# Reading a result back into SBUF for two output blocks, and a new instruction order for a two-branch spectral kernel on one core

## The chip, the cores and the metric

One core of a Trainium2 chip runs the whole kernel. The metric is the device time of one execution in microseconds (us). The core has five engines with a queue each: TensorE (PE in the profile; PEld is its weight load), VectorE (DVE), ScalarE (ACT), GpSimd (POOL) and SyncE (SP), which here only issues DMA transfers. Each queue is worked off in the order in which the program was written. An instruction whose inputs are not there holds up all that stand behind it in its queue.

## The reference

Two branches work on sequences of 2048 steps by 640 channels and are mixed by a gate:

```python
x = A_q
g = _sigmoid((x * gate_w).sum(-1, keepdims=True))
# branch A: short convolution of k (4 taps), times v, long causal convolution with ssm_k by FFT, times q
k_shift = sum over 4 taps of k_pad[:, t:t + S, :] * shift_k
kv = k_shift * v
y = irfft(rfft(kv, 2 * S) * rfft(ssm_k, 2 * S))[:S] + kv * ssm_D
a = q * y
# branch B: two-dimensional FFT of the input, times a complex filter, and back
b = irfft2(rfft2(x) * (w_r + 1j * w_i))
return g * a + (1 - g) * b
```

Branch B takes `x = A_q` as its input too. Everything is float32.

## The kernel before, in words

All Fourier transforms are written as matmuls with constant matrices, in two stages each, with a 32x32 block transpose on DVE (`STREAM_TRANSPOSE`) that moves each stage's result from PSUM back to SBUF. The work is cut into units, and a unit's name with its number and the number of the step in it names every instruction below (`afin9.4` is step 4 of unit 9 of `afin`).

- **Start of branch B.** `fwd` (8 units, lines 286 to 319) folds one eighth of the input by four additions in SBUF (steps 1, 2 at L295 and 3, 4 at L297), multiplies it on PE (L303, L310), and ACT brings the result back into XX. `gcol` (L278 to L282) makes the gate's columns by five tiny DVE operations; every `fwd` matmul waits for it. `gate` (L328) gathers the gate when all eight `fwd` are done. `b1` (10 units, L348, L352) is the first stage of the long transform.
- **Middle of branch B.** `bs2` (8 units, L369 to L379) is the second stage: two matmul groups, four DVE products with the filter w (L374), two combining additions (L378). Each unit loads its w into one of two L buffers. `i1` (6 units) and `u` (16 units) go back, and `dic` (8 units, L430 to L458) ends branch B: matmuls, scaling by 1-g on ACT, four additions in SBUF (L448, L450), and two transfers to the output: columns 0 to 383 are added onto what branch A has stored there (an accumulating transfer, issued by POOL, L454), columns 384 to 639 are stored plainly by SP (L457).
- **Branch A** goes by five column blocks c = 0 to 4. `kv` (10 units, two a block) makes kv (PE L469, DVE L472, two additions L478, a transpose L481), `h` (10 units) loads the filter (an accumulating load, L489) and adds the D term (L491), `s1Y` and `s1H` are first stages (L509, L519), `s2` (20 units, four a block) multiplies spectra (PE L539, ACT L544, products L557 and L560, for blocks 1 and 3 additions L565), `is1` goes back (L265, L270), and `afin` (10 units, two a block, L582 to L613) ends it: PE L600, one product with g times q (L606, from PSUM on DVE), and the output.

Blocks 0, 1, 2 of branch A are stored first and branch B is added onto them. For blocks 3 and 4 it is the other way: branch B is stored first (L457), and each of the four `afin` units 6 to 9 adds its 512 KB by an accumulating transfer that POOL issues (L612).

Three tables set everything that is free. `ORDER` is the order in which the planned operations are written, and so the order in each queue. `ON_DVE` names the SBUF operations made by `ttop` that go to DVE; the others go to POOL. `SLOTS` gives each buffer its place in its pool (five V, four M, three T, two L, two H, one G, eight PSUM banks). The durations handed to `op` and the `kb` are read by nothing in the program:

```python
with tc.manual_schedule():
    for i in ORDER:
        plan.ops[i].fn()
```

Of the kernel before, what the change touches and what calls it, by code (L numbers as in the profile page):

```python
# [7 lines left out]
OP = mybir.AluOpType  # L8
# [17 lines left out]
    "bs2": [(7, 8)],
    "s2": [(3, 4), (4, 9), (4, 11), (6, 4), (7, 4), (7, 9), (8, 9), (9, 9), (10, 9), (12, 4), (12, 9), (13, 4), (13, 9), (14, 4), (14,
        9), (14, 10), (14, 11), (15, 4), (15, 9), (16, 4), (16, 9), (17, 4), (17, 9), (19, 4)],
    "afin": [(0, 4), (1, 4), (3, 4), (4, 4), (5, 4), (6, 4), (7, 4), (8, 4), (9, 4)],
    "dic": [(0, 6), (0, 8), (1, 6), (1, 7), (1, 8), (2, 6), (2, 9), (4, 6), (4, 7), (4, 8), (4, 9), (5, 6), (5, 8), (5, 9), (7, 7)],  # L30
    "kv": [(7, 5), (8, 5), (9, 5)],
# [713 lines left out]
```

## Time and profile before

| | us |
|---|---|
| median of three runs | 324.7 (319.17, 324.7, 324.92) |
| the profiled execution, its own time | 325.14 |
| its span, first to last instruction | 323.3 |
| PE busy | 259.7 (80% of the span) |
| DVE busy | 237.7 (73%) |
| POOL busy | 160.6 (50%) |
| ACT busy | 103.7 (32%) |
| mean granted PE clock | 0.946 |

The time is 1.84 us longer than the span in the profiled execution. A group in the profile is named by its line, engine and operation, then output and inputs by buffer name; a bracket behind an instruction in the timeline is the idle time just before it and what ended it.

### The profile page before, as it was taken

What the parts mean: (1) busy time and instruction counts of PE and PEld (TensorE: products, weight loads), DVE (VectorE), ACT (ScalarE), POOL (GpSimd) and SP (SyncE); (2) the same over time, 40 slices, a digit from 0 to 9 for tenths busy, and PEclk for the clock granted to TensorE, in tenths of its full rate; (3) what the DMA queues carried; (4) which work ended last, traced back from release to release, by engine and by line L of the source; (5) the groups of instructions that cost most, each with busy time, mean ns of one, the idle gap of its engine ahead of it and who ended that gap; (6) DMA issues with size and microseconds to landing.
All of it is one profiled execution on the core that took longest, in us unless ns stands there. A gap on an engine that the chain in (4) does not pass through costs nothing. (4 is left out here: it accounts for less than half of the span.)

```text
span 323.3 us, 10329 instructions
## 1 busy us (share of the span) xinstructions
PE 259.7 (80%) x4626; PEld 151.5 (47%) x4626; DVE 237.7 (73%) x241; ACT 103.7 (32%) x233; POOL 160.6 (50%) x120
## 2 busy tenths in 40 slices
PE   0399979988989769887669589888999987999920
...
DVE  2919965988989798998867697227846878797730
...
GB/s 291 418 415 358 396 274 35 310 415 258 39 153 317 149 131 3 2 188 356 256 152 191 138 2 212 307 143 243 233 107 129 178 160 109 67 74 14 2 148 112
DMA packets 26172, 60.49 MB, mean 187 GB/s; under 512 B 1680, under 2 KB 16400, under 8 KB 24464
## 3 DMA queue, kind: packets, MB, share of 16 engines
...
q8 instruction: 36, 0.59, 0.7%
q14 instruction: 8, 0.07, 0.1%
...
## 5 line engine op out<-in xcount | busy, mean ns | idle before, releaser
L519 DVE STREAM_TRANSPOSE YY<-banks 128x1024 f32<-128x1024 f32 x40 | 48.2, 1229 | 11.5 <-PE banks L509 11.5
L539 PE MATMUL banks<-YY,s2a 64*32 64x256 f32 x1280 | 46.7, 417 | 9.3 <-DVE M L557 4.0
L478 POOL TENSOR_TENSOR T<-V 128x512 f32<-128x512 f32 x13 | 18.2, 1436 | 45.9 <-DVE V L472 45.9
L539 PEld LDWEIGHTS banks<-YY,s2a 64*32 64x32 f32 x1280 | 25.9, 110 | 31.2 <-DVE YY L519 7.6
L544 ACT ACTIVATE H<-banks 128x512 f32<-128x512 f32 x40 | 23.9, 598 | 39.5 <-PE banks L539 30.6
L303 PE MATMUL banks<-cc,XX 128*64 128x162 f32 (+1 forms) x256 | 22.7, 325 | 14.6 <-DVE cc L282 12.2
L590 ACT ACTIVATE V<-V,g 128x128 f32<-128x128 f32 x72 | 22.0, 389 | 38.1 <-DMA V<-q 26.8
L265 PE MATMUL banks<-YY,ca 32*64 32x512 f32 x512 | 33.2, 607 | 0.8 <-DVE YY L519 0.5
L557 POOL TENSOR_TENSOR YY<-YY,H 128x512 f32<-128x512 f32 x15 | 19.6, 1315 | 17.8 <-ACT H L544 13.0
L303 PEld LDWEIGHTS banks<-cc,XX 128*64 128x64 f32 x256 | 19.0, 147 | 20.0 <-POOL XX L297 12.7
L270 DVE STREAM_TRANSPOSE YY<-banks 128x2048 f32<-128x2048 f32 x10 | 23.1, 2310 | 5.1 <-PE banks L265 5.1
L374 DVE TENSOR_TENSOR M<-banks,L 128x642 f32<-128x642 f32 x32 | 24.4, 813 | 2.8 <-DMA L<-w 2.7
L600 PE MATMUL banks<-YY,is2a 128*64 128x128 f32 x320 | 21.3, 291 | 4.8 <-DVE YY L270 2.5
L600 PEld LDWEIGHTS banks<-YY,is2a 128*64 128x64 f32 x320 | 19.5, 143 | 10.0 <-DVE YY L270 4.0
L472 DVE TENSOR_TENSOR V<-banks,V 128x1024 f32<-128x1024 f32 x10 | 12.1, 1210 | 15.4 <-DMA V<-v 6.7
L265 PEld LDWEIGHTS banks<-YY,ca 32*64 32x64 f32 x512 | 14.6, 129 | 17.9 <-issue 10.7
L430 PE MATMUL banks<-di,L 128*128 128x160 f32 x128 | 20.6, 316 | 2.5 <-ACT L L419 2.4
L378 POOL TENSOR_TENSOR XX<-M,M 128x642 f32<-128x642 f32 x15 | 19.8, 1384 | 5.2 <-DVE M L374 3.4
L297 POOL TENSOR_TENSOR XX<-M 128x640 f32<-128x640 f32 x10 | 18.3, 1842 | 7.8 <-DVE M L295 7.5
L430 PEld LDWEIGHTS banks<-di,L 128*128 128x128 f32 x128 | 18.5, 198 | 7.2 <-ACT L L419 4.7
L419 ACT ACTIVATE L<-banks 128x640 f32<-128x640 f32 x16 | 11.1, 703 | 33.0 <-PE banks L411 28.9
L348 PE MATMUL banks<-XX,cb 128*128 128x512 f32 (+1 forms) x42 | 20.6, 629 | 1.3 <-DVE M L557 1.0
...
## 6 DMA issues: line engine op xcount, KB each, us to landing
...
V<-v SPq DMA_DIRECT2D x10, 512.0 KB, 7.4
V<-h SPq DMA_DIRECT2D x10, 512.0 KB, 7.0
V<-h POOLq DMA_DIRECT2D x10, 512.0 KB, 8.3
V<-q SPq DMA_DIRECT2D x10, 512.0 KB, 4.8
out_dram<-V SPq DMA_DIRECT2D x6, 512.0 KB, 5.7
```

The source lines that it names most:

```text
L265: mm(p[h * 64:h * 64 + 64, j, :nd * 8], is1[r, sg, ri, :], v[r, h * 2 + src, :, d0:d0 + nd, :].rearrange("p m d e -> p d m e"), start=(i = ...
L270: nc.vector.transpose(by_col(x, d0, nd), p[:, :, :nd * 8].rearrange("p j (d i) -> p d j i", i=8))
L303: mm(bk(p, g_)[ri * 64:ri * 64 + 64, o:o + n], X[:, s, g_ * 64:g_ * 64 + 64], df[:, 0, ri * 323 + o:ri * 323 + o + n], start=(o == 0), sto ...
L348: mm(v()[:, e0:e0 + ne], m1b, by_col(XX, d0 + e0, ne), start=True, stop=True)
L374: op("DVE", dve(642), lambda x=x, t=t, ri=ri, p=p: tt(T(t)[:, ri], ps(p)[:, :, :NC], sb(w_, 2, 2, NC)[:, x], op=OP.mult), r=[p, w_], w=[t] ...
L378: ttop(642, lambda f, ri=ri, o=o, dst=dst: f(dst(), T(t1)[:, ri], T(t2)[:, 1 - ri], op=o), r=[t1, t2], w=xe + [("XS", m, e, ri)])
L430: mm(bk(p, b)[:, n * 160:n * 160 + 160], U[:, t_, r_], di[:, b * 160:b * 160 + 160], start=(n == 0), stop=False)
L519: op("DVE", dve(1024), lambda b=b: nc.vector.transpose(by_col(YY[:, :, y], a * 64 + b * 32, 32), view(b)), r=[p[b]], w=yk)
L539: mm(ps(p)[j * 32:j * 32 + 32, h].rearrange("p (y r d) -> p y r d", y=2, r=2)[:, :, ri], s2a[r, k, ri * 32:ri * 32 + 32], YY[r, k // 2, y0 ...
L544: op("ACT", act_us(512), lambda p=p, hs=hs: act(sb(hs, 2, 256), ps(p)[:, :, 256:], AF.Copy), r=[p], w=[hs])
L590: act(dst(j), src(j), AF.Copy, scale=g[:, n0 + j:n0 + j + 1])
L600: mm(v()[b * 64:b * 64 + 64, j, :], is2a[:, n2, :], row(YY[:, :, yp], n2), start=True, stop=True)
```

## The change

For two of the last four `afin` units (7 and 9, the second halves of blocks 3 and 4) the accumulating transfer goes. Instead SP reads back what branch B has stored (512 KB into a V buffer), DVE adds it in SBUF, and SP stores the sum plainly. Units 6 and 8 keep the accumulating transfer. `ON_DVE`, `ORDER` and `SLOTS` are all new. Of the SBUF additions, DVE now has 24 of the 32 of `fwd` (16 before), 6 of the 16 of `kv` (3), 16 of the 32 of `dic` (15), 9 of the 16 combining ones of `s2` (3), and none of `bs2` (1). The other edits to numbers are durations that nothing reads.

```diff
 ON_DVE = {(n, i, k) for n, l in {
-    "fwd": [(0, 1), (1, 1), (1, 2), (1, 3), (1, 4), (2, 1), (2, 4), (3, 4), (4, 1), (4, 2), (5, 1), (6, 1), (6, 4), (7, 1), (7, 2), (7,
-        4)],
...
+    "fwd": [(0, 1), (0, 2), (0, 3), (1, 1), (1, 2), (1, 3), (1, 4), (2, 1), (2, 2), (2, 3), (2, 4), (3, 1), (3, 3), (3, 4), (4, 1), (4,
+        4), (5, 3), (6, 1), (6, 3), (6, 4), (7, 1), (7, 2), (7, 3), (7, 4)],
...
+    "afin": [(0, 4), (2, 4), (3, 4), (4, 4), (5, 4), (6, 4), (7, 4), (7, 6), (8, 4), (9, 4), (9, 6)],
...
+BACK={7,9}
...
         if c < FIRST:
             op("SP", ISS, lambda: dma(out[:, n0:n0 + 8, cs], Q()), r=[qt], w=[("oA", c, n0 // 8)], kb=524)
+            return
+        ob = [("oB", v) for v in range(n0 // 2, n0 // 2 + 4)]
+        if 2 * c + n0 // 8 in BACK:
+            bt = new("V")
+            op("SP", ISS, lambda: dma(sb(bt, 8, 128), out[:, n0:n0 + 8, cs]), r=ob, w=[bt], kb=524)
+            ttop(1024, lambda f: f(sb(qt, 1024), sb(qt, 1024), sb(bt, 1024), op=OP.add), r=[bt], w=[qt])
+            op("SP", ISS, lambda: dma(out[:, n0:n0 + 8, cs], Q()), r=[qt, bt], kb=524)
         else:
-            op("POOL", 1.4, lambda: nc.gpsimd.dma_start(out[:, n0:n0 + 8, cs], Q(), accum_op=OP.add),
-               r=[qt] + [("oB", v) for v in range(n0 // 2, n0 // 2 + 4)], kb=800)
+            op("POOL", 1.6, lambda: nc.gpsimd.dma_start(out[:, n0:n0 + 8, cs], Q(), accum_op=OP.add), r=[qt] + ob, kb=1150)
```

The lines of the changed program stand two to three higher up to `kv` and `s2` (L295 is L297, L297 is L299, L374 is L376, L606 is L609), and the accumulating transfer of `afin` is L622.

Three places show what the new order does. First the start of the DVE queue. Before, `gcol` (`cc` and `gt`) stands behind the first addition of each of two units:

```order
L295 TENSOR_TENSOR M_64<-XX 128x640
L295 TENSOR_TENSOR M_65<-XX 128x640
L278 TENSOR_SCALAR cc<-cc 128x8
L279 TENSOR_TENSOR gt<-cc 128x2x2
L280 TENSOR_TENSOR gt<-cc 128x2x2
L281 TENSOR_TENSOR cc<-gt 128x2x2
L282 TENSOR_TENSOR cc<-gt 128x2x2
L297 TENSOR_TENSOR XX<-M_64 128x640
```

In the changed program the first unit (`fwd6`) is folded as far as DVE does it ahead of `gcol`:

```order
L297 TENSOR_TENSOR M_64<-XX 128x640
L297 TENSOR_TENSOR M_65<-XX 128x640
L299 TENSOR_TENSOR XX<-M_64 128x640
L297 TENSOR_TENSOR M_66<-XX 128x640
L299 TENSOR_TENSOR XX<-M_64 128x640
L280 TENSOR_SCALAR cc<-cc 128x8
L281 TENSOR_TENSOR gt<-cc 128x2x2
L282 TENSOR_TENSOR gt<-cc 128x2x2
L283 TENSOR_TENSOR cc<-gt 128x2x2
L284 TENSOR_TENSOR cc<-gt 128x2x2
L297 TENSOR_TENSOR M_66<-XX 128x640
```

Three more additions and the wait for one more input stand ahead of `gcol` now; POOL's queue holds one addition of `fwd6` and then one of `fwd0`, which needs DVE additions that stand behind `gcol`.

The second place is DVE in `bs2`, at the first reuse of an L buffer. Before, from the last product of `bs22` (buffer L_63) to the first of `bs21` in the same buffer, with all of `bs20` (L_62), two `s2` products and one long transpose (L270) between:

```order
L374 TENSOR_TENSOR M_65<-banks,L_63 128x642
L560 TENSOR_TENSOR YY<-banks,H_77 128x4x128
L374 TENSOR_TENSOR M_66<-banks,L_62 128x642
L560 TENSOR_TENSOR YY<-banks,H_76 128x4x128
L374 TENSOR_TENSOR M_66<-banks,L_62 128x642
L374 TENSOR_TENSOR M_67<-banks,L_62 128x642 x2
L270 STREAM_TRANSPOSE YY<-banks 128x64x16x2
L374 TENSOR_TENSOR M_64<-banks,L_63 128x642 x2
```

In the changed program the same stretch goes from the last product of `bs20` (L_62) to the first of `bs21` in that buffer:

```order
L376 TENSOR_TENSOR M_66<-banks,L_62 128x642
L376 TENSOR_TENSOR M_65<-banks,L_63 128x642
L563 TENSOR_TENSOR YY<-banks,H_76 128x4x128
L376 TENSOR_TENSOR M_65<-banks,L_63 128x642
L376 TENSOR_TENSOR M_67<-banks,L_63 128x642 x2
L376 TENSOR_TENSOR M_64<-banks,L_62 128x642
```

Four products of the other buffer and one `s2` product now stand between two uses of one buffer.

The third place is the end of the DVE queue, `is1` (L270, L272) and the four `afin` units. Before:

```order
L557 TENSOR_TENSOR YY<-banks,H_77 128x4x128
L270 STREAM_TRANSPOSE YY<-banks 128x64x16x2 x3
L606 TENSOR_TENSOR V_68<-banks,V_68 128x1024
L606 TENSOR_TENSOR V_69<-banks,V_69 128x1024
L606 TENSOR_TENSOR V_71<-banks,V_71 128x1024
L606 TENSOR_TENSOR V_70<-banks,V_70 128x1024
```

In the changed program (L619 is the new addition):

```order
L609 TENSOR_TENSOR V_68<-banks,V_68 128x1024
L272 STREAM_TRANSPOSE YY<-banks 128x64x16x2 x2
L609 TENSOR_TENSOR V_70<-banks,V_70 128x1024
L619 TENSOR_TENSOR V_70<-V_70,V_69 128x1024
L609 TENSOR_TENSOR V_71<-banks,V_71 128x1024
L609 TENSOR_TENSOR V_72<-banks,V_72 128x1024
L619 TENSOR_TENSOR V_72<-V_72,V_68 128x1024
```

And the end of SP's queue there, behind the last loads of q (L589) and branch B's plain stores (L459):

```order
L589 DMA V_72<-q 128x1024
L459 DMA out_dram<-M_65 128x2x256
L459 DMA out_dram<-M_66 128x2x256
L618 DMA V_69<-out_dram 128x8x128
L618 DMA V_68<-out_dram 128x8x128
L620 DMA out_dram<-V_70 128x8x128
L620 DMA out_dram<-V_72 128x8x128
```

`afin6` has moved ahead of the last two transposes, and the read-back for unit 9 goes into V_68, the buffer from which `afin6` is sent by its accumulating transfer.

More of the change, by code (lines that the diff above doesn't have):

```diff
@@ L23 @@
 ON_DVE = {(n, i, k) for n, l in {
-    "fwd": [(0, 1), (1, 1), (1, 2), (1, 3), (1, 4), (2, 1), (2, 4), (3, 4), (4, 1), (4, 2), (5, 1), (6, 1), (6, 4), (7, 1), (7, 2), (7,
-        4)],
[L26 to L31, printed above, removed]
+    "fwd": [(0, 1), (0, 2), (0, 3), (1, 1), (1, 2), (1, 3), (1, 4), (2, 1), (2, 2), (2, 3), (2, 4), (3, 1), (3, 3), (3, 4), (4, 1), (4,
[4 rows of a table added]
+    "afin": [(0, 4), (2, 4), (3, 4), (4, 4), (5, 4), (6, 4), (7, 4), (7, 6), (8, 4), (9, 4), (9, 6)],
+    "kv": [(3, 5), (6, 4), (6, 5), (7, 5), (9, 4), (9, 5)],
+    "dic": [(0, 6), (0, 7), (0, 8), (0, 9), (1, 6), (1, 7), (1, 8), (2, 7), (3, 6), (3, 7), (3, 8), (4, 6), (4, 9), (7, 6), (7, 7), (7,
+        9)],
 }.items() for i, k in l}
@@ L204, in _body, with ttop @@
     dma = nc.sync.dma_start
-    dve = lambda n: 0.157 + 1.04e-3 * n
-    dvs = lambda n: 0.2 + 1.4e-3 * n
-    act_us = lambda n: 0.17 + 0.83e-3 * n
-    pool_us = lambda n: 0.38 + 1.95e-3 * n
+    dve = lambda n: 0.07 + 1.035e-3 * n
+    act_us = lambda n: 0.06 + 0.86e-3 * n
+    pool_us = lambda n: 0.16 + 2.13e-3 * n
     mmu = lambda n: 1.667e-3 * n
-    ISS = 0.45
-    def ttop(n, fn, alt=None, pre=None, **kw):
-        o = op("POOL", pool_us(n), None, **kw)
-        o.alt, o.pre = alt or dvs(n), [(x, on, x.us) for x, on in pre or ()]
+    ISS = 0.43
+    def ttop(n, fn, alt=None, pre=None, us=None, **kw):
+        o = op("POOL", us or pool_us(n), None, **kw)
+        o.port = (1, 1 if alt is None else 0)
+        o.alt, o.pre = alt or dve(n), [(x, on, x.us) for x, on in pre or ()]
         dv_ = o.key in ON_DVE
@@ L282, in f @@
             tt(df[:, :, 322:324], gt[:, :, 0::2], gt[:, :, 1::2], op=OP.subtract)
-        op("DVE", 0.5, f, w=DF)
+        op("DVE", 0.9, f, w=DF).port = (0, 1)
     def fwd(u):
@@ L330, in gate @@
         op("PE", 0.2, pe, r=[("lg", u, a) for u in range(8) for a in range(2)] + ["cb"], w=[p], mode="128x64")
-        op("ACT", 1.5, lambda: act(g, ps(p)[:, 0, :16], AF.Sigmoid), r=[p], w=["g"])
+        op("ACT", 0.25, lambda: act(g, ps(p)[:, 0, :16], AF.Sigmoid), r=[p], w=["g"])
         op("ACT", 0.2, lambda: act(om, g, AF.Copy, scale=-1.0, bias=1.0), r=["g"], w=["om"])
@@ L384, in i1 @@
         p = new("ps", 4)
-        op("PE", 1.16 * 2 * mmu(nd * 8), lambda: inv1(ps(p), [(XX, 0, 0, 0), (XX, 1, 0, 1)], d0, nd), r=[("XS", m, e, ri) for m in range(4) for e in range(2) for ri in range(2)] + ["ca"],
+        op("PE", 1.06 * 2 * mmu(nd * 8), lambda: inv1(ps(p), [(XX, 0, 0, 0), (XX, 1, 0, 1)], d0, nd), r=[("XS", m, e, ri) for m in range(4) for e in range(2) for ri in range(2)] + ["ca"],
            w=[p], mode="32x64")
@@ L416, in both @@
             rest()
-        op("PE", 1.48, both, r=[("XI", u) for u in range(6)] + [("is2b", n // 8), ("is2b", 2 + n // 8)], w=[p] if n % 2 else [p, ub], mode="u")
+        op("PE", 1.37, both, r=[("XI", u) for u in range(6)] + [("is2b", n // 8), ("is2b", 2 + n // 8)], w=[p] if n % 2 else [p, ub], mode="u")
         op("ACT", act_us(640), lambda: act(sb(ub, 2, 640)[:, n % 2], ps(p).rearrange("p a b -> p (a b)")[:, :640], AF.Copy), r=[p], w=[ub])
@@ L437, in rest @@
                        tile_position=(b * 32, 0))
-        op("PE", 2.37, pe, r=[ub, "di"], w=p, mode="F")
-        op("PE", 0.755, rest, r=[ub, "di"], w=p, mode="32x128")
+        op("PE", 2.1, pe, r=[ub, "di"], w=p, mode="F")
+        op("PE", 0.6, rest, r=[ub, "di"], w=p, mode="32x128")
         E = lambda: sb(e_, 2, 2, 2, 160)
@@ L453, in dic @@
         if nf:
-            op("POOL", 1.4, lambda: nc.gpsimd.dma_start(out[:, n0:n0 + 2, :nf], sb(bf, 2, 640)[:, :, :nf], accum_op=OP.add),
-               r=[bf] + [("oA", c, v // 4) for c in range(FIRST)], kb=1024)
+            op("POOL", 0.9, lambda: nc.gpsimd.dma_start(out[:, n0:n0 + 2, :nf], sb(bf, 2, 640)[:, :, :nf], accum_op=OP.add),
+               r=[bf] + [("oA", c, v // 4) for c in range(FIRST)], kb=nf * 2.3)
         if nf < D:
```

35 lines of the change are left out of this document (18 added, 17 removed), and 81 rows, old and new, of tables (ON_DVE, ORDER, SLOTS).

## The prediction

> **What bounds the kernel now.** I read the page's busy slices first, then the timeline where PE idles, then the waits of DVE.
>
> ```profile
> PE 259.7 (80%) x4626; PEld 151.5 (47%) x4626; DVE 237.7 (73%) x241; ACT 103.7 (32%) x233; POOL 160.6 (50%) x120
> PE   0399979988989769887669589888999987999920
> DVE  2919965988989798998867697227846878797730
> ```
>
> PE is the bound nearly everywhere, with DVE close behind it in the middle (slices 11 to 20). No PE work is added or removed, so the forecast is about PE's 64 us without work: 12.2 at the start, 14 at the end, some 37 between. The start:
>
> ```profile
> 4.68 0.83 DVE L295 TENSOR_TENSOR M<-XX 128x640 f32<-128x640 f32 x1 [4.68 <-DMA XX<-xT]
> 6.23 1.36 DVE L295 TENSOR_TENSOR M<-XX 128x640 f32<-128x640 f32 x1 [0.72 <-DMA XX<-xT]
> 8.13 0.88 DVE L278 TENSOR_SCALAR cc<-cc 128x8 f32<-128x8 f32 x1 [0.54 <-DMA cc<-df]
> 8.94 1.52 POOL L295 TENSOR_TENSOR M<-XX 128x640 f32<-128x640 f32 x1
> 9.04 1.45 DVE L279 TENSOR_TENSOR gt<-cc 128x4 f32<-128x4 f32 x1
> 10.59 1.50 DVE L281 TENSOR_TENSOR cc<-gt 128x4 f32<-128x4 f32 x1
> 12.02 0.15 DVE L282 TENSOR_TENSOR cc<-gt 128x4 f32<-128x4 f32 x1
> 12.20 0.77 PE L303 MATMUL banks<-cc,XX 128*64 128x162 f32 x2 [12.20 <-DVE cc L282]
> 14.30 4.43 PE L303 MATMUL banks<-cc,XX 128*64 128x162 f32 x30 [1.33 <-DVE XX L297]
> ```
>
> Four elements a partition take DVE 0.15 us (L282), but 1.45 when a POOL addition began just before (L279 beside POOL's from 8.94 to 10.46; L281 lies beside the next one): the DVE operation ends when POOL's does. So the two engines hold each other up when both add in SBUF. `gcol` takes 4.0 us for that reason, and the first matmul waits for it. The same happens until 41 us:
>
> ```profile
> L297 DVE TENSOR_TENSOR XX<-M x6: 782/2108/4392, 12.1 to 48.4; 128x640 f32<-128x640 f32 x6
> 42.18 3.80 PE L509 MATMUL banks<-T,ca 32*32 32x512 f32 x56 [1.98 <-DVE V L472]
> 49.00 2.35 PE L509 MATMUL banks<-T,ca 32*32 32x512 f32 x64
> 40.00:45.00 5.00, 3.02 (x59) 0.95 (x56) 3.37 (x3) 0.82 (x3) 2.30 (x2) 0.74 1.01 282
> 56.95 0.24 PE L328 MATMUL banks<-lg,cb 128*64 128x16 f32 x2 [0.18 <-DVE YY L519]
> ```
>
> One DVE addition that takes 0.78 us at the least took 4.39; `kv`'s product and transpose stood behind it, PE idled 1.98 us, and then 56 matmuls took 3.80 us where 64 take 2.35, at a granted clock of 0.74 (seventh number of the window row). `gate` came at 56.95.
>
> **Term 1, start to `gate`.** Before: PE's work in its queue up to there is eight `fwd` of 2.43 + 0.81, three `kv` of 1.09, two double `s1Y` of 2.35 and one `s1H` of 1.25, together 35.1 (rows below for what is not above).
>
> ```profile
> 19.40 2.43 PE L303 MATMUL banks<-cc,XX 128*64 128x162 f32 x32
> 21.77 1.09 PE L469 MATMUL banks<-G,gd 64*32 64x512 f32 x16
> 22.79 0.81 PE L310 MATMUL banks<-cc,XX 32*64 32x162 f32 x32
> 54.38 1.25 PE L509 MATMUL banks<-V,ca 32*32 32x512 f32 x32
> ```
>
> From 12.2 to 56.95 are 44.75 us, so 9.65 were lost: 2.8 on the slow first group (0.77 + 4.43 for 2.43), 1.33 behind it, 1.98 + 1.75 at 42 (3.80 for 56/64 of 2.35), 1.8 in small gaps. After: the gate's input df is fourth in the queue instead of third. Landings come 1.55 us apart here (4.68, 6.23), df's was at 8.1, so it is there near 9.5. `gcol` then takes 5 x 0.15, since POOL's next addition needs DVE work that stands behind `gcol`: PE starts at 10.3. If POOL interferes after all, it is 12.2 again or later; if df lands in its old place, 9.4. Up to `gate` PE has 32.8 us (two `kv`, one double `s1Y`, one folded of 1.15, one `s1H`). I leave it the slow first group, the small gaps and 1 us of waiting for the second unit, 5.6, and let the loss at 42 go, as DVE has 24 `fwd` additions of 0.8 but is no longer held. What is late next there is the input itself, still 1.5 us a unit. `gate` at 48.7, 8.25 earlier, of which 2.3 are PE work moved behind it: **-6.0** (bounds: -1.9, the start alone, and -9.6, all of the loss).
>
> The Trainium skill (TensorE: Matmul & The Clock Gate, "What's actually happening") says that the clock halves only after an idle window of about 3.4 us. Here it was lower after 1.98 us, so the trace does not agree. By that rule the 1.75 would not hang on the idle time and would be lost here or elsewhere, and the sum below would be 317.3.
>
> **Term 2, `gate` to the first `bs2`.** The same products in another mix. DVE gets some 3 us more, from shares and from moved `s1Y` work; PE has work beside it. I take **0**, from -3 (the idle times of PE around 105 to 120 go) to +5 (DVE's own additions all end on the path).
>
> **Term 3, `bs2`.** Two L buffers; a load is issued when the buffer's last product is done, and DVE waits if it lands late:
>
> ```profile
> 145.28 6.12 DVE L374 TENSOR_TENSOR M<-banks,L 128x642 f32<-128x642 f32 x8
> 152.48 0.68 DVE L560 TENSOR_TENSOR YY<-banks,H 128x512 f32<-128x512 f32 x1
> 153.80 3.03 DVE L374 TENSOR_TENSOR M<-banks,L 128x642 f32<-128x642 f32 x4 [0.64 <-DMA L<-w]
> 158.82 3.03 DVE L374 TENSOR_TENSOR M<-banks,L 128x642 f32<-128x642 f32 x4 [0.80 <-DMA L<-w]
> 163.15 0.83 DVE L374 TENSOR_TENSOR M<-banks,L 128x642 f32<-128x642 f32 x1 [1.30 <-DMA L<-w]
> 148.30 3.46 SPq L358 DMA_DIRECT2D L<-w x2
> 156.86 0.33 SPq L358 DMA_DIRECT2D L<-w x1
> DMA to landing us min/median/max: 3.8/5.9/10.7
> ```
>
> The last row is that of the L buffers. The three waits cost 2.7 us. From issue to use went 5.5 us (148.30 to 153.80) and 6.3 (156.86 to 163.15). Of the six reuses in the changed order two have four products (6.12/8 = 0.77 each) and one `s2` product (0.68) between, 3.7 us; two have 4.4; two have 6 and more. At 5.5 and 0.1 to issue, DVE waits 1.9 + 1.9 + 1.2 + 1.2 = 6.2, less the 2.7 that go. But other waits lengthen the gaps (0.9 us stand beside them in these rows), so I take **+2.7**. From the least landing (3.8) it is -2.3; from 7.4 it is +12, and the largest, 10.7, would give +29.
>
> **Term 4, `u` and `dic`.** PE lost time there behind `s2` of block 3, which waits for M buffers and for POOL's combining:
>
> ```profile
> 265.33 1.16 PE L539 MATMUL banks<-YY,s2a 64*32 64x256 f32 x32 [1.17 <-DVE M L557]
> 267.37 1.80 PE L539 MATMUL banks<-YY,s2a 64*32 64x256 f32 x32 [0.88 <-DVE M L557]
> 270.50 3.67 PE L539 MATMUL banks<-YY,s2a 64*32 64x256 f32 x64 [1.33 <-DVE M L557]
> L565 POOL TENSOR_TENSOR YY<-M,M x13: 1275/1282/1897, 109.3 to 279.0; 128x512 f32<-128x512 f32 x13
> L565 DVE TENSOR_TENSOR YY<-M,M x3: 686/693/1482, 112.7 to 267.9; 128x512 f32<-128x512 f32 x3
> ```
>
> Idle 3.4 and slow groups 2.1 (1.80 and 3.67 against 1.16 for 32). In the new order these `s2` units stand between `dic` units, and seven of their eight combining additions run on DVE at 0.69 instead of 1.28 on POOL, two of them there before. The gain is at most 5.5; the loss is at most DVE's five more additions, 3.5, if DVE is late. I take **-2**.
>
> **Term 5, the end.**
>
> ```profile
> 309.30 1.23 DVE L606 TENSOR_TENSOR V<-banks,V 128x1024 f32<-128x1024 f32 x1 [0.59 <-PE banks L600]
> 310.82 1.54 POOL L612 DMA_DIRECT2D out_dram<-V  x1 [0.27 <-DVE V L606]
> DMA to landing us min/median/max: 2.1/5.2/10.7
> out_dram<-V SPq DMA_DIRECT2D x6, 512.0 KB, 5.7
> out_dram<-V POOLq DMA_DIRECT2D x4, 512.0 KB, 9.0
> V<-q SPq DMA_DIRECT2D x10, 512.0 KB, 4.8
> ```
>
> The row of landings is that of the output. PE ends at P = 309.3, where the last product starts; the last of four accumulating transfers is issued at 310.8, and the span ends at P + 14.0; with the longest landing (10.7) 1.8 us lie behind it. After: `afin9.4` ends at P + 1.25, the addition takes 1.2 (not in the trace; 1024 elements from PSUM take 1.23, 640 in SBUF 0.78; bounds 0.8 and 2.8, behind one POOL issue of 1.54), the plain store 5.7 and the rest 1.8: P + 9.9, **-4.1**. The accumulating transfer of `afin8` goes out at P - 0.4 and at 9.0 lands at P + 8.6, before the store's at P + 8.1 or hardly after. The read-back for unit 9 waits for `afin6`'s transfer, as it uses its buffer: `afin6.4` ends some 14 us ahead of the last addition (two long transposes of 2.3, PE's `is1` beside them, three `afin`), and 9.0 + 4.8 = 13.8 is just in time. With 10.7 it is 1.6 late. Bounds -6 (a store of 3.8) and +0.5.
>
> **Sum.** -6.0 + 0 + 2.7 - 2 - 4.1 = -9.4, from the profiled 325.14 to 315.7; that execution stands 0.4 above the median, so 315.5.
>
> **Rivals.**
> - *The clock is lost anyway.* The lower clock may not be a price of the short idle time at 42 us; then the 1.75 of term 1 is paid here or at another place, 317.3. For it: the start's slow group (4.43 for 2.43) has no short idle time before it. Against it: 0.74 right behind the 1.98 us. 6%. The Trainium skill (TensorE: Matmul & The Clock Gate) would have it so, as 1.98 us are under its window.
> - *The turns are not taken.* The queues run freely; an order fixes no turn between two engines. If DVE and POOL drift by one operation (1.5 us), the additions of `fwd` collide as before (L297's median of 2.1 against 0.8, six times, is 8 us of DVE), and term 1 is -1.9: 319.6. For it: DMA landings set the beat until 45 us. Against it: POOL has only 8 of 32 additions left. 20%.
> - *The filter loads become the bound (slower).* Place: DVE at the reuse of L_62 and L_63. If loads take 7.4 us or more, the four short gaps cost 3.8 + 3.8 + 3.1 + 3.1 and the longer ones 1.5, +12 instead of +2.7, 325: no gain. At 9 us it is +20, 333. It decides from 7.4 on; the row's median is 5.9, its maximum 10.7. 12%.
> - *The middle gains too.* Of the 37 us that PE idles between 12.2 and 309.3, some 5 lie ahead of `gate`; most of the others stand behind DVE. If a third of them goes with the collisions (L565 on DVE took up to 1.48 us instead of 0.69), it is 305. 20%.
> - The forecast, 309 to 319: 42%.
>
> **How the numbers follow.** The range leaves out the worse half of the third rival and the tails of the fourth: 303 to 327. Two per cent, about what a measurement of this kernel can tell from no change, is 318.2 and 331.2. Faster: most of the forecast (0.34), half the first rival, a fifth of the second, all of the fourth, 0.61. Slower: most of the third, 0.11. Within: 0.28.
>
> **What would show it.** Term 1: the first matmul near 10.3 us, L280 to L284 at 0.15 us each, `gate` near 49, L299 on DVE at 0.8. Term 3: DVE's waits for L<-w, more than 2.7 us in total. Term 4: no PE idle time over 1 us at `s2` of block 3. Term 5: the span's end 8 to 11 us behind the last matmul, and DVE's L619 waiting for V<-out_dram by under 2 us. I am wrong if the V buffers, one of which holds unit 9's v early, keep SP's queue back, since everything behind the waiting load comes late too.

## The result and the profile after

| | before | after |
|---|---|---|
| median, us (lowest to highest, runs) | 323.56 (319.17 to 324.92, 4) | 301.34 (300.57 to 302.55, 4) |
| the profiled execution, its span | 325.14, 323.3 | 300.57, 298.8 |
| mean granted PE clock in it | 0.946 | 0.986 |

The changed kernel takes 0.940 of the time (95% interval 0.930 to 0.950). The forecast was 315.5, with a range of 303 to 327: the direction was right, and 14 us are missing. A ratio with its interval leaves out the runs that lie over 1.5% above the fastest of their kernel; the kernel of before spreads by more than that (316 to 333 us in all comparisons), so the medians of all runs stand beside the ratios.

The rows of the page of after that answer to those shown of before, with its row of the granted clock (the share of full speed that PE's clock is given, in tenths; 9 is 90% or more):

```profile
PE 251.6 (84%) x4626; PEld 148.4 (50%) x4626; DVE 241.0 (81%) x259; ACT 102.9 (34%) x234; POOL 135.6 (45%) x102
PE   0698779999988989576799899978999989999970
DVE  2959983999988799998999997248976798899491
PEclk9999999999999999999999999979999999999996
```

The clock row of the page of before:

```profile
PEclk9999979999999979999979799979999995999975
```

PE does the same work in 8.1 us less busy time. The clock is enough for that: before, six slices ahead of the end stand at 7 or 5, after, one. By the clock's records PE was busy for 22.1 us at half speed before and for 3.4 us after, and half of such busy time is extra. The prediction named one of the six dips, at 42 us; the slow groups at that of 267 us it counted in term 4, without the clock.

The start of after, DVE and then PE:

```profile
9.60 0.17 DVE L280 TENSOR_SCALAR cc<-cc 128x8 f32<-128x8 f32 x1
10.15 0.16 DVE L284 TENSOR_TENSOR cc<-gt 128x4 f32<-128x4 f32 x1
10.29 4.28 PE L305 MATMUL banks<-cc,XX 128*64 128x162 f32 x32 [10.29 <-DVE cc L283]
```

`gcol` is as cheap as forecast, and the first matmul comes at 10.3. The additions of `fwd` still collide at times, by the row of their line:

```profile
L299 DVE TENSOR_TENSOR XX<-M x13: 780/815/2375, 7.3 to 40.5; 128x640 f32<-128x640 f32 x13
```

Their median is 0.8 us now, the largest 2.4 (before 2.1 and 4.4).

Time by stage: from the first matmul to `gate`, to the first `bs2`, to the first `u`, to PE's end, to the span's end. The columns are the length, the busy time of PE, PEld, DVE, ACT and POOL, the granted clock, and the DMA share and rate. Before:

```profile
12.20:56.95 44.75, 40.17 (x721) 26.03 (x721) 31.40 (x25) 13.79 (x34) 22.81 (x14) 0.96 0.82 306
56.95:129.78 72.83, 63.38 (x1091) 28.57 (x1091) 63.97 (x67) 26.09 (x58) 36.77 (x31) 0.98 0.65 196
129.78:200.22 70.44, 55.76 (x1056) 26.39 (x1057) 59.26 (x62) 17.07 (x46) 31.69 (x24) 0.95 0.52 170
200.22:309.26 109.04, 100.36 (x1767) 70.45 (x1760) 75.61 (x82) 45.45 (x94) 58.99 (x43) 0.95 0.58 134
309.26:323.30 14.04, 0.00 (x0) 0.00 (x0) 1.23 (x1) 0.00 (x0) 2.84 (x2) 0.60 1.12 137
```

After:

```profile
10.29:49.69 39.40, 34.50 (x672) 25.16 (x673) 30.00 (x30) 12.80 (x34) 17.29 (x10) 1.00 1.03 386
49.69:118.75 69.06, 64.03 (x1138) 28.19 (x1138) 63.29 (x69) 25.57 (x58) 31.99 (x26) 1.00 0.65 196
118.75:183.16 64.41, 52.62 (x1060) 25.41 (x1057) 60.75 (x61) 18.25 (x48) 32.61 (x25) 1.00 0.55 188
183.16:290.24 107.08, 100.45 (x1762) 69.63 (x1760) 79.88 (x90) 44.99 (x95) 49.97 (x37) 0.98 0.66 150
290.24:298.80 8.56, 0.00 (x0) 0.00 (x0) 2.45 (x2) 0.00 (x0) 1.40 (x1) 0.72 0.87 163
```

`gate` comes 7.3 us earlier, with 2.3 us of PE work moved behind it; the second stage gains 3.8 in spite of that work, `bs2` 6.0, `u` to PE's end 2.0, the end 5.5.

### The profile page after: what moved, and what is told of

It reads as the page before. It is cut to its first block, busy times and chain, and to the rows that moved or that the text cites. A ratio compares the mean times of both kernels' runs of the same rounds, so it can differ in the third digit from the quotient of the medians.

```text
span 298.8 us, 10323 instructions
## 1 busy us (share of the span) xinstructions
PE 251.6 (84%) x4626; PEld 148.4 (50%) x4626; DVE 241.0 (81%) x259; ACT 102.9 (34%) x234; POOL 135.6 (45%) x102
## 4 chain that ended last, share of the span: by engine, by line
PE 38%; DVE 27%; DMA 22%; issue 6%; POOL 2%; ACT 2%; SPq 0%; DVEq 0%; POOLq 0%; ACTq 0%
DMA V<-h 12%; PE banks L267 9%; PE banks L542 8%; PE banks L512 6%; DVE M L376 5%; DVE YY L272 5%; DMA XX<-xT 4%; DVE YY L522 4%; PE banks L432 3%; PE banks L350 3%; PE banks L603 3%; DMA cc<-df 2%; PE banks L405 2%; DVE M L563 2%; DMA V<-v 2%
## 5 line engine op out<-in xcount | busy, mean ns | idle before, releaser
L542 PE MATMUL banks<-YY,s2a 64*32 64x256 f32 x1280 | 41.8, 390 | 5.2 <-DVE M L376 3.3
L480 POOL TENSOR_TENSOR T<-V 128x512 f32<-128x512 f32 x10 | 13.6, 1372 | 56.8 <-DVE V L474 56.8
L542 PEld LDWEIGHTS banks<-YY,s2a 64*32 64x32 f32 x1280 | 24.2, 105 | 23.3 <-DVE M L376 5.5
L305 PE MATMUL banks<-cc,XX 128*64 128x162 f32 (+1 forms) x256 | 21.5, 321 | 11.6 <-DVE cc L283 10.3
L272 DVE STREAM_TRANSPOSE YY<-banks 128x2048 f32<-128x2048 f32 x10 | 22.9, 2304 | 5.8 <-PE banks L267 5.8
L305 PEld LDWEIGHTS banks<-cc,XX 128*64 128x64 f32 x256 | 19.2, 146 | 15.2 <-DVE cc L283 10.3
L380 POOL TENSOR_TENSOR XX<-M,M 128x642 f32<-128x642 f32 x16 | 21.8, 1387 | 10.6 <-DVE M L376 10.5
L376 DVE TENSOR_TENSOR M<-banks,L 128x642 f32<-128x642 f32 x32 | 24.8, 812 | 1.7 <-DMA L<-w 1.2
L560 POOL TENSOR_TENSOR YY<-YY,H 128x512 f32<-128x512 f32 x16 | 21.0, 1328 | 4.6 <-ACT H L547 2.5
L603 PEld LDWEIGHTS banks<-YY,is2a 128*64 128x64 f32 x320 | 18.0, 134 | 8.5 <-DVE YY L272 3.8
L452 POOL TENSOR_TENSOR M<-M 128x640 f32<-128x640 f32 x10 | 16.4, 1638 | 11.8 <-DVE M L450 8.2
L405 PE MATMUL banks<-cc,XX 128*128 128x128 f32 x128 | 19.5, 295 | 2.2 <-DVE YY L522 1.4
L491 POOL DMA_DIRECT2D V<-h x10 | 8.9, 889 | 26.4 <-ACT V L490 26.4
```

The costliest lines, as they stand in the source:

```text
L272: nc.vector.transpose(by_col(x, d0, nd), p[:, :, :nd * 8].rearrange("p j (d i) -> p d j i", i=8))
L305: mm(bk(p, g_)[ri * 64:ri * 64 + 64, o:o + n], X[:, s, g_ * 64:g_ * 64 + 64], df[:, 0, ri * 323 + o:ri * 323 + o + n], start=(o == 0), sto ...
L376: op("DVE", dve(642), lambda x=x, t=t, ri=ri, p=p: tt(T(t)[:, ri], ps(p)[:, :, :NC], sb(w_, 2, 2, NC)[:, x], op=OP.mult), r=[p, w_], w=[t] ...
L380: ttop(642, lambda f, ri=ri, o=o, dst=dst: f(dst(), T(t1)[:, ri], T(t2)[:, 1 - ri], op=o), us=1.28, r=[t1, t2], w=xe + [("XS", m, e, ri)])
L405: mm(psa[:, t, :, b, :], row(XX, n2)[:, t * 161:t * 161 + 128], W(n2), start=True, stop=True)
L542: mm(ps(p)[j * 32:j * 32 + 32, h].rearrange("p (y r d) -> p y r d", y=2, r=2)[:, :, ri], s2a[r, k, ri * 32:ri * 32 + 32], YY[r, k // 2, y0 ...
```

## The experiments

**Theories.** A: the gain is that of the new order and of the new shares together, each as priced in the terms, only larger. B: a part of it is the clock, which the kernel of before loses again and again because PE idles, and which the changed kernel keeps. C (rival to B): the lowered clock lies beside DVE's work and costs nothing.

**Shares and order apart.** Each of these kernels takes one set of shares (`ON_DVE`) and one order.

```diff
 # order_only: the changed kernel
-ON_DVE = (its own)
+ON_DVE = (that of before; the additions of the read-back stay on DVE)
 # shares_only: the kernel of before
-ON_DVE = (its own)
+ON_DVE = (that of after, without the additions of the read-back)
 # late_shares: the changed kernel
-ON_DVE for s2 12 to 19 and dic = (its own)
+ON_DVE for s2 12 to 19 and dic = (that of before)
```

> The changed kernel's order, buffers and read-back, but with the shares of before (which additions run on DVE and which on POOL). Theory (the order carries the middle, the shares the start): the start loses part of its gain, since POOL adds beside DVE again in fwd, gate near 52 to 55 us instead of 49.7; the bs2 stage keeps its 64 us (before: 70.4); total 305 to 310. Rival (the shares carry it): the gain is mostly gone, 315 or more. Rival (the shares are worth nothing): 300 to 303.

Measured: 318.75 us (10 runs; before 322.98, ratio 0.989, 0.985 to 0.993).

> The order of before with the new shares, no read-back. Theory (the order carries the middle): 318 to 326, the bs2 stage still near 70 us and DVE later in u and dic, where it now does POOL's additions in an order made for others. Rival (the shares carry it): 308 to 314, with DVE's fwd additions at 0.8 us and gate near 50.

Measured: 325.0 us (10 runs; before 322.98, ratio 1.009, 1.003 to 1.015).

> The changed kernel with the shares of before in the last part alone: s2 of blocks 3 and 4 and all of dic (30 of these additions and multiplications on DVE instead of 36, and partly others). Theory (the order carries the start and bs2, the shares the last part): from u to PE's end 113 to 120 us instead of 107, all up to u as in the changed kernel, total 308 to 315. Rival (the shares of the start and of the first blocks matter as much): under 306.

Measured: 311.23 us (4 runs; before 325.31, ratio 0.977, 0.962 to 0.993).

So the new shares alone lose 0.9%, the order with its read-back alone gains 1.1%, and both gain 6.0%: neither is worth much without the other. By the medians, the old shares in the last part alone cost 9.9 us against the changed kernel, all others 7.5 more. Expected of `order_only` were 305 to 310; it missed mainly since the last part needs its shares, as the stage from `u` to PE's end shows (109.0 us before, 107.1 after). In `order_only`, with the stage from `gate` to `bs2` ahead:

```profile
49.93:124.36 74.43, 67.36 (x1148) 28.09 (x1139) 63.27 (x67) 23.89 (x50) 32.16 (x27) 0.95 0.60 180
190.34:310.93 120.59, 102.48 (x1762) 71.44 (x1760) 76.31 (x84) 44.90 (x95) 58.10 (x43) 0.96 0.59 133
```

and the last part alone in `late_shares`:

```profile
182.04:299.42 117.38, 101.55 (x1762) 70.75 (x1760) 73.86 (x84) 44.74 (x95) 58.42 (x43) 0.97 0.61 136
```

Of the waits of `late_shares` in that part, the row that bears on it (the wait in all, times, the longest):

```profile
DVE M L559 <- POOL YY L564: 8.8, 2, 5.0
```

The combining additions of `s2` on POOL hold the M buffers, and DVE's next product waits 8.8 us for them. In the changed kernel DVE does them itself, where it would have waited: DVE is busy 79.9 us of 107.1 there, against 73.9 of 117.4. `gate` stands at 49.9 us in `order_only`, which has the shares of before, and at 50.5 in `shares_only`, which has the order of before: for the start either is enough. `bs2` itself takes 66.0 us in `order_only`. The stage from `gate` to `bs2` is short only with both (74.4 us with the order alone, 78.4 with the shares alone, 69.1 with both), though two lowered stretches of the clock lie in the 74.4 and one in the 78.4. In `shares_only`:

```profile
50.46:128.85 78.39, 63.53 (x1090) 27.98 (x1090) 64.92 (x70) 27.17 (x64) 34.16 (x28) 0.98 0.62 182
```

**The read-back.** Undone in the changed kernel, put alone into the kernel of before, and there for unit 9 alone into a buffer that is free early:

```diff
 # no_back: the changed kernel, the accumulating transfers at the places of the addition and the store
-BACK={7,9}
+BACK=set()
 # back_only and back9: the kernel of before
+BACK={7,9}   # back9: {9}
```

> The changed kernel without the read-back: units 7 and 9 add into the output by an accumulating transfer again, at the place of their addition or store. Term 5 of the prediction: the span's end goes from 8.6 us behind the last matmul to about 14, total 304 to 307. Rival (the accumulating transfer is only as late as the store): within 1 us of the changed kernel, 300 to 302.5.

Measured: 304.82 us (4 runs; ratio to before 0.945, 0.938 to 0.952), 3.5 more than the changed kernel by the medians; the span ends 11.75 us behind PE's end.

> The kernel of before with the read-back alone for units 7 and 9; all else stands in its order. Term 5: the span's end goes from 14 us behind the last matmul to 8.5 to 10, total 318 to 320 against 323.6. Rival (unit 9's read-back waits for unit 6's accumulating transfer and comes late): DVE waits over 2 us for the read-back and the total stays at 322 to 325.

Measured: 320.87 us (4 runs; before 322.98, ratio 0.984, 0.974 to 0.994). The end did not gain: the span ends 14.3 us behind PE's end, for unit 9's addition waits for its read-back:

```profile
308.51 1.23 DVE L616 TENSOR_TENSOR V<-V,V 128x1024 f32<-128x1024 f32 x1 [7.21 <-DMA V<-out_dram]
```

> The kernel of before with the read-back for unit 9 alone, into a V buffer that has been free since s1H 8, so that it waits for no accumulating transfer; unit 7 accumulates as before. Term 5 (the end is worth 4 us by the plain store of the last unit): the read-back lands before the last product, the span ends 9.5 to 11 us behind PE's end instead of 14, total 319 to 320 against 323. Rival (the store has to wait for the accumulating transfers of units 7 and 8 in the queues): 12 to 14 us, total 321 to 324.

Measured: 319.79 us (10 runs; before 325.31, ratio 0.998, 0.985 to 1.011). The span ends 12.0 us behind PE's end, 2 less than before.

So the end gains 5.5 us in the changed kernel, of which 3.2 go with the read-back, and 0 or 2 in the order of before. The landings show why (least, median, largest). The four accumulating transfers at the end of before:

```profile
DMA to landing us min/median/max: 6.3/9.0/10.7
```

The four of `no_back`:

```profile
DMA to landing us min/median/max: 6.3/6.9/8.5
```

The two that are left in after:

```profile
DMA to landing us min/median/max: 6.1/6.2/6.2
```

The plain store of unit 9 in `back9`, behind three accumulating transfers:

```profile
DMA to landing us min/median/max: 8.3/8.3/8.3
```

The two plain stores at the end of after:

```profile
DMA to landing us min/median/max: 3.2/4.1/5.0
```

In these rows an accumulating transfer that goes out ahead of the others, or alone, lands in 6.1 to 6.3 us. Four that go out 1.6 to 1.8 us apart land about 3 us apart, the last after 10.7, and a plain store behind three of them takes 8.3 instead of 3.2 to 5.0. The changed kernel has two, 12 us apart, because `afin6` now stands ahead of `is1` 8 and 9; that also gives unit 9's read-back its buffer in time.

**The clock.** Stretches of 3.41 us, a pair for each of three of the lowered ones, in before (length, PE busy; the clock is the third number from the end):

```profile
38.95:42.36 3.41, 1.43 (x40) 0.34 (x40) 3.38 (x3) 1.55 (x4) 3.33 (x2) 1.00 0.99 310
42.36:45.77 3.41, 3.41 (x56) 0.77 (x36) 1.04 (x1) 0.00 (x0) 0.02 (x1) 0.50 1.03 305
161.83:165.24 3.41, 1.15 (x32) 0.51 (x32) 2.11 (x5) 1.66 (x5) 2.62 (x2) 1.00 0.75 259
165.24:168.65 3.41, 3.29 (x32) 3.28 (x32) 2.23 (x4) 1.64 (x3) 0.90 (x1) 0.50 0.26 101
178.89:182.31 3.42, 1.02 (x16) 0.24 (x16) 2.86 (x3) 0.00 (x0) 0.00 (x0) 1.00 0.49 198
182.31:185.72 3.41, 3.04 (x40) 1.25 (x48) 2.14 (x2) 2.45 (x8) 0.00 (x0) 0.50 0.02 5
```

and in after, one that kept its clock, and its one lowered pair:

```profile
37.95:41.36 3.41, 1.86 (x79) 0.94 (x74) 3.35 (x4) 1.51 (x4) 0.94 (x1) 1.00 1.04 314
194.96:198.38 3.42, 1.67 (x25) 1.38 (x26) 0.64 (x2) 2.54 (x6) 0.97 (x2) 1.00 1.01 290
198.38:201.79 3.41, 3.41 (x14) 3.41 (x14) 2.26 (x3) 0.94 (x2) 0.00 (x0) 0.50 1.01 249
```

The lowered stretches begin whole multiples of 3.413 us apart (42.36 to 165.24 are 36 of them), and each, but for one that follows another lowered one, follows a stretch of the same grid in which PE was busy for less than half: 1.02 to 1.43 of 3.41 before, 1.67 after; with 1.86 the clock stayed. To test it, useless matmuls on a scratch tile, written to PSUM columns that nobody reads, stand in the idle times of the kernel of before:

```diff
+def fill(bank, c0, n, times):
+    for _ in range(times):
+        mm(banks[:64, bank, c0:c0 + n], scr[:, :64], scr[:, 64:64 + n], start=True, stop=True)
 # before_fill: inside s1Y 1 and behind s2 7, s2 9, i1 5, dic 2; before_fill2: the first one ahead of s1Y 1
 # before_fill3: as before_fill2, half as many; fill_busy: as many as before_fill2, behind fwd 7, fwd 3, i1 4, u 5, u 7
```

> The kernel of before with useless matmuls at five places where PE sat idle: behind the first half of s1Y 1 (42 us), behind s2 7 (114), s2 9 (163), i1 5 (181) and dic 2 (209). They read a scratch tile, write columns of PSUM that nobody reads, and add about 5 us of PE work inside idle times of 1.2 to 2.4 us. Theory (the clock is judged over fixed stretches of 3.41 us, and one in which PE works under half the time is followed by one at half speed): three to five of the seven lowered stretches go, each is worth up to 1.7 us, 315 to 320 against 323. Rival (the lowered clock follows from something else, or costs nothing since DVE is the bound): the lowered stretches stay or the total does, 322 to 326.

Measured: 322.09 us (4 runs; before 323.38), above the 315 to 320 expected. The first filler missed its idle time and ran behind it, in the lowered stretch, 3.85 us on the path:

```profile
43.98 3.85 PE L251 MATMUL banks<-scr 128*64 128x160 f32 x16
```

> The first filled kernel again, with the one filler that stood behind its idle time moved ahead of it: the useless matmuls at 40 us now follow the second product of fwd 5, in front of s1Y 1, so that they lie inside the wait. The other four as before. Theory (a stretch of 3.41 us with PE under half busy halves the clock of the next, and the slow work lies on the path): one or two lowered stretches left instead of seven, gate at 55.5 to 57 instead of 60.0, total 3 to 6 us under the kernel of before. Rival (DVE sets the pace, the slow work is hidden): total within 1.5 us of before, although the stretches are gone.

Measured: 317.72 us (12 runs, 316.12 to 320.84; before 325.31, 23 runs, 316.49 to 332.96). The ratio is 0.999 (0.993 to 1.006): the best four runs of before are as fast. A filler takes 2.4 us, twice what had been meant:

```profile
39.52 2.39 PE L251 MATMUL banks<-scr 128*64 128x160 f32 x16
```

With the 1.87 us of the fourth they are 11.4 us of useless work, and the median is 7.6 us lower.

> The kernel of before with the same amount of useless matmuls as in the filled kernel, but behind five products where PE goes on without a gap (fwd 7 at 34 us, fwd 3 at 54, i1 4 at 197, u 5 at 203, u 7 at 235). Theory (fillers help only where they lift a stretch over half busy): the lowered stretches of before stay, five to seven of them, and the total is that of before or up to 5 us more, 323 to 330. Rival (any added work or another timing breaks the pattern that costs the time): 316 to 320, as with the fillers in the idle times.

Measured: 323.04 us (13 runs; before 323.40, 17 runs; ratio 1.010, 1.004 to 1.016). The same amount of work at other places gains nothing. As a control it is weak: its profile (327.97 us) has three lowered stretches and not the five to seven expected, and the useless work lies on the path here.

> The filled kernel of before with half of the useless matmuls at each of the five places, 5.7 us in all, so that each fills about half of its idle time. Theory: a place with 2.0 to 2.4 us of idle time keeps about 1 us of it, its stretch stays over half busy and the clock up; 314 to 317, as fast as with the double fillers or up to 3 us faster. Rival (half is too little, other small idle times in the same stretch bring it under half): some stretches come back, 318 to 322.

Measured: 316.33 us (6 runs; before 324.78, 11 runs; ratio 0.976, 0.970 to 0.982): 8.4 us less by the medians, with 6.2 us of useless work in it. Its clock row on the page:

```profile
PEclk9999999999999999999999999999999996999975
```

Its stages:

```profile
12.29:56.18 43.89, 39.98 (x729) 27.09 (x729) 31.41 (x25) 13.76 (x34) 22.86 (x14) 1.00 0.83 311
56.18:126.62 70.44, 62.97 (x1099) 28.86 (x1099) 63.52 (x67) 26.20 (x58) 36.76 (x31) 1.00 0.67 203
126.62:190.99 64.37, 55.08 (x1076) 26.38 (x1076) 58.75 (x61) 17.31 (x46) 31.70 (x24) 1.00 0.58 186
190.99:301.13 110.14, 100.56 (x1776) 70.12 (x1768) 75.83 (x83) 45.22 (x94) 58.95 (x43) 0.97 0.58 133
301.13:315.10 13.97, 0.00 (x1) 0.00 (x0) 1.23 (x1) 0.00 (x0) 2.82 (x2) 0.58 1.12 137
```

Only the dip at 259 us is left, where no filler stands. So the fillers do take lowered stretches away, and the kernel with them takes 0.976 of the time. But not all of that can be put down to the clock. Of the 8.2 us by which the two profiles differ 6.1 lie in `bs2`, and there the order of before stands in five more profiles. Its rows in `back9`, which has no fillers and one lowered stretch there (at 162 us, much as before has one at 165), and in `fill_busy`:

```profile
127.85:192.34 64.49, 54.31 (x1057) 26.43 (x1057) 58.56 (x61) 17.28 (x46) 31.74 (x24) 0.97 0.56 185
130.41:201.45 71.04, 56.85 (x1080) 26.33 (x1081) 58.51 (x61) 17.31 (x46) 31.68 (x24) 0.95 0.53 169
```

`back_only`, also with one lowered stretch there, takes 64.8 us, `before_fill` and `before_fill2`, with none, 65.6 and 65.4. Only before (70.4) and `fill_busy` are long, and in these two DVE waits for the filter `h` of branch A, with PE behind it. The row of before, then that of `fill_busy`:

```profile
179.45 0.21 DVE L491 TENSOR_TENSOR V<-V,gd 128x32 f32<-128x32 f32 x1 [2.96 <-DMA V<-h]
179.53 0.21 DVE L505 TENSOR_TENSOR V<-V,gd 128x32 f32<-128x32 f32 x1 [5.31 <-DMA V<-h]
```

The accumulating load of `h` that POOL issues there is late in both. Its landing in before, in `fill_busy` and in `back9`:

```profile
DMA to landing us min/median/max: 9.2/9.2/9.2
DMA to landing us min/median/max: 10.8/10.8/10.8
DMA to landing us min/median/max: 5.6/5.6/5.6
```

In the five other profiles of this order (`back_only`, `back9` and the three filled ones) it lands after 5.4 to 5.6 us, and POOL issues it 1.1 to 1.9 us ahead of the first of two 512 KB loads (`cc<-is2b`) of SP. In before it goes out 0.4 us ahead of that load, in `fill_busy` 0.3 behind it. That these loads are what delays it is a reading; no run sets the order of the issues on purpose. A lowered clock is not needed for it: `fill_busy` had its full clock from 20 us up to this wait, and the lowered stretch at 182 us of before comes after it. Against `back9`, DVE in before waits 3.0 us more for `h` and 1.3 more for w, of 5.95 us in all; 1.5 us in which it waits for PE, at half speed behind the first wait, are among the rest.

So B holds in that the clock falls where PE idles, but the larger part of the difference between these two profiles is the wait for `h` and what follows it, and C is not refuted everywhere. With one lowered stretch the start takes 44.8 us (`back9`) and 44.0 (`back_only`), without 43.9 (`before_fill3`); `gate` to `bs2` takes 72.8 with one, and 70.4, 70.8 and 72.2 without (`back_only`, `back9`, `fill_busy`); `u` to PE's end takes 109.0 with three and 108.4 with none (`back_only`). Whether the fillers win their 2.4% by the clock or by the turn of that load is not separated, since one execution of each kernel has a trace.

**The clock in the changed kernel.** Useless matmuls ahead of its first product, or at its barest stretches:

```diff
 # after_warm: ahead of all else
+plan.fill(7, 0, 160, 24)
 # after_fill: behind u 2 and dic 2; after_fill3: fewer there, and behind fwd 4 and fwd 7 as well
```

> The changed kernel with 24 useless matmuls on a scratch tile ahead of the first product, from about 1 to 8 us, while PE waits for its first input. Theory (PE starts at half speed until one stretch of 3.41 us has been busy): the first fwd group takes 2.4 us instead of 4.28, gate comes 0.5 to 1.9 us earlier, total 299.5 to 301. Rival (the first group is slow for its inputs): it stays at 4.28 and the total at 301.3, or up to 1 us later if the useless matmuls run past 10.3 us.

Measured: 300.74 us (4 runs). PE's first group in its timeline:

```profile
10.45 2.50 PE L319 MATMUL banks<-cc,XX 128*64 128x162 f32 x32 [0.83 <-DVE cc L297]
```

It takes 2.50 us instead of 4.28, so the slow first group is PE's start at half speed and not its inputs; the records of the full clock begin at 14.06 us in after and at 4.47 here. But `gate` came at 49.5 instead of 49.7: PE waited for the rest again on the way.

> The changed kernel with useless matmuls at its one lowered stretch: eight behind u 2 (196.4 us, 1.75 us of idle time) and four behind dic 2 (204.2 us, 1.1 us). Theory: no lowered stretch between the first fwd and the end, dic 2's matmuls take 2.44 us instead of 4.12, total 1 to 1.7 us under 301.3. Rival (hidden behind DVE or ScalarE): 301 to 301.6.

Measured: 301.46 us (6 runs).

> The changed kernel with small fillers (0.9 to 1.2 us each) at its four barest stretches: behind fwd 4 (32.6 us) and fwd 7 (38.4), u 2 (196.4) and dic 2 (204.2). Theory: its one lowered stretch goes, worth at most 1.7 us, and the others were not lowered: 299.5 to 301. Rival (DVE sets the pace there): 301 to 302.

Measured: 303.73 us (7 runs, 297.37 to 305.56); three lowered stretches lie in its profile, where none was expected. One of them lies in `bs2`, which takes 64.4 us with it, as in the changed kernel without. None of these three kernels differs from the changed kernel by more than its own spread.

**What a lowered stretch costs there.** Waits put into PE's queue. In the first two the wait's matmul wrote columns that the next product uses, so that these two kernels spoil their result, and PE waited behind it once more; in the last two, shown here, it writes columns that nobody reads:

```diff
+def stall(bank, c, n):
+    act(scr[:, :1], banks[:, bank, :1], AF.Copy)
+    for _ in range(n): act(scr, scr, AF.Copy)
+    mm(banks[:32, bank, c:c + 1], scr[:, :32], scr[:, 64:65], start=True, stop=True)
```

> The changed kernel with five waits of about 2.6 us put into PE's queue (behind b1 3, is1 4, i1 2, u 0, is1 8): a small matmul waits for a chain of ScalarE copies on a scratch tile. Theory (a stretch of 3.41 us with PE under half busy lowers the clock of the next): three to five lowered stretches behind them, 13 us of waits and 4 to 7 of slow work, less what DVE's slack takes: 4 to 7 us more than the same waits in halves. Rival (only the sum of the idle time counts): the same total as with ten halves, within 1.5 us.

> The changed kernel with ten waits of about 1.3 us in PE's queue, the five places of the kernel with long waits and five more, each 3.8 us or more behind the one before. The same idle time in all. Theory: at most one or two lowered stretches more than the changed kernel, 4 to 7 us less than with five long waits. Rival (only the sum counts): the same total, within 1.5 us.

Measured: 324.19 and 327.98 us (4 runs each). PE idled up to 2.4 us more behind a half wait, so the halves were no halves, and these two tell nothing of the price.

> The changed kernel with three waits of about 2.5 us in PE's queue, behind i1 2, u 0 and dic 7: a one-column matmul into columns of PSUM that nobody reads waits for a chain of five ScalarE copies. Theory: two or three lowered stretches more than in the changed kernel, each of which costs up to 1.7 us: 7.5 us of waits, less DVE's slack, and 3 to 5 us for the clock, 308 to 313; 3 to 5 us more than with six halves. Rival (only the sum of the idle time counts): the same as with six halves, within 1.5 us.

> The changed kernel with six waits of about 1.3 us, behind i1 2, i1 5, u 0, u 5, dic 7 and u 10: the same idle time as three whole ones. Theory: none or one lowered stretch more than in the changed kernel, 305 to 309. Rival (only the sum counts): the same as with three whole ones, within 1.5 us.

Measured: 309.81 and 309.99 us (6 runs each). The waits were 2.7 us each in the one and 1.5 to 1.7 in the other, 8.1 and 9.2 in all, with five lowered stretches against two in the profiles (of the longest execution of each). The totals are the same, as the rival has it; with 1.1 us more of waits in the halves a price of some 1 us for three stretches would be hidden in it. In the changed kernel the price of a lowered stretch stays open; for three it is small beside the expected 3 to 5 us.

## Why the prediction was wrong, point by point

The terms against what was measured, from the stage rows. The middle column is the profiled run of before against before_fill3, which has the order of before without five of its seven lowered stretches, with 6.2 us of useless work, and with the load of `h` in time; the 2.3 us of work moved behind `gate` are taken out of term 1 and put into term 2, as the prediction had it.

| term | forecast | before to before_fill3 | before_fill3 to after | in all |
|---|---|---|---|---|
| 1, start to `gate` | -6.0 | -0.8 | -4.2 | -5.0 |
| 2, `gate` to `bs2` | 0 | -2.4 | -3.7 | -6.1 |
| 3, `bs2` | +2.7 | -6.1 | 0 | -6.0 |
| 4, `u` to PE's end | -2 | +1.1 | -3.1 | -2.0 |
| 5, the end | -4.1 | -0.1 | -5.4 | -5.5 |
| sum (rounded once) | -9.4 | -8.2 | -16.3 | -24.5 |

- **Term 3 is the step that failed**, by 8.7 us, and its mistake is in the price of before. It took the 70.4 us of the one profiled execution for what the order costs, and priced one kind of wait in them, 2.7 us for the loads of w. DVE also waited 3.0 us for `h` there, whose load took 9.2 us, and PE ran at half speed behind that wait; where this load lands in 5.4 to 5.6 us the order of before takes 64.4 to 65.6. The new order loads no `h` in this stage, and takes 64.4. The wait stood among DVE's waits of before, and the term has nothing for it. The profiled execution (325.14) lies above all four timed runs beside it. Why the load was late stays open.
- The waits for the filter loads, the term's own subject, went the other way by less. DVE's waits for the L buffers in after, and the landings of these loads:

```profile
  DMA L<-w: 1.2, 1
DMA to landing us min/median/max: 3.9/4.0/5.7
```

  They land in 4.0 us in the median, not in the 5.5 that I carried over, and cost 1.2 us in one wait instead of 2.7 in three. The row of landings that I used held all eight loads of the kernel; the six of this stage took 3.8 to 7.3 us before. The short gaps were there; at the least landing my own sum gave -2.3, and -1.5 came. That is observed, and no run isolates why the loads are faster.
- **Term 2** was taken as 0 because DVE would get 3 us more. DVE's busy time went from 64.0 to 63.3, PE's idle time from 9.5 to 5.0. The order of before without a lowered stretch takes 70.4 to 72.2 us here, so at most 2.4 of the 6.1 are its dip at 117 us. The runs with one half of the change each (74.4 and 78.4 us) say that shares and order have to fit; which of the stage's operations does it was not tried, and the cause of this term stays open.
- **Term 1** was right: the first matmul at 10.29 (forecast 10.3), `gcol` at 0.16 to 0.17 us an operation, `gate` at 49.7 (48.7). One reading in it was wrong. The slow first group is still there (4.28 us for 2.43) and is not worth removing: with PE warm before it `gate` came 0.2 us earlier.
- **Term 4** was right in size (-2.0). The late shares are worth 9.9 us when taken away, far more than that: order and shares are a pair here.
- **Term 5** was too small by 1.4. The last plain store landed after 5.0 us, not 5.7, and the span ended 1.0 us behind it, not 1.8. The two accumulating transfers took 6.2 us, not 9.0. The condition that I named, unit 9's read-back just in time behind `afin6`, decides: in the order of before it is 7.2 us late and the gain is nothing.
- **The rivals.** "The middle gains too" (305, 20%) came nearest, but its mechanism, collisions in SBUF, is not what the rows of `bs2` show: that was the wait for `h`, with a lowered clock behind it. "The clock is lost anyway" was wrong: with one lowered stretch instead of seven it is mostly kept. The Trainium skill (TensorE: Matmul & The Clock Gate, "What's actually happening") gives a free-running window of 3413 ns; the grid of 3.413 us here agrees. Its condition, an idle window, does not: PE was busy 0.30 to 0.42 of the stretches ahead. I had cited the rule against the trace, and did not ask what else in a window of that length could explain 1.98 us.
- **The sum** has a slip of 0.2: 0.4 under 315.7 is 315.3.

## What to carry to other kernels

A stage's length in one profile is that of one execution. Before a term is priced from it, list every wait in the stage, also those for loads that the change does not aim at, and compare with a second profile of the same order: here it was 70.4 us in one and 64.5 in another. A dip in the row of the granted clock marks a place where PE idled; look for what it waited for before giving the clock a price. Where two engines share the additions, order and shares are one choice; each alone was worth about 1% or less than nothing here, both 6%. Accumulating transfers that go out close together landed later here; spread them, or take some away, before counting on the end of the last.

## What the runs showed that had not been expected

In the 19 profiles, on the grid of 3.413 us up to PE's last matmul, 50 of some 1500 stretches at full clock were followed by one at half. PE was busy at most 0.54 of those, and at least 0.46 of all that kept the clock. Of 62 lowered stretches 12 were followed by another: those were busy up to 0.83, and the ones that gave the clock back at least 0.76. So in these runs the clock falls below about half, and comes back only above some three quarters.

Before spread by 16 us in 23 runs, the same kernel with 11.4 us of useless work in its idle times by 5 in 12. The clock is not the whole reason for the spread: of the runs of before on record one took 318.26 us at a mean granted clock of 0.943, and another 330.37 at 0.955. A load that lands late in some executions, as that of `h` in two of seven profiles, is a candidate that no run here tests over many executions.
